# Placing a pair's late tiles over the last tile's y, leaving one attention slot empty, and re-pacing background steps in a fused attention, MoE and MoE kernel

## The chip, the core and the metric

One core of a Trainium2 chip runs the whole program. The metric is the device time of one execution in microseconds (us), median of several executions.

## The reference

Attention over short windows, then two feed-forward blocks in a row, all in float32:

```python
# attention: 4 x 8 heads, 768 positions, 64 wide; chunks of 32 see 16 left, 8 right, 8 memory keys
scores = scale * q_c @ k_full.T; a = exp(scores - max); out = (a / sum) @ v_full
x = out as [3072 tokens, 512]
# first MoE block (512 -> 1536 -> 512)
xn = x / rms(x) * rms_g
x = (silu(xn @ w_gate) * (xn @ w_val)) @ w_out
# second MoE block (512 -> 2048 -> 512)
h = x @ w_in;  g = h if h >= 1, 0 if h <= -1, else (h + 1)**2 / 4
return g @ w_out
```

## The kernel before

The 3072 tokens are six tiles of 512. A float32 product is made of three matmuls on operands split into a high and a low part, so nearly all of TensorE's work comes in threes.

Part one: a hand-written order of attention for the first tile. Part two: the first MoE block for tiles 0 to 3, one at a time (the loop over t, lines 793 to 822). For each of 12 blocks f of the hidden width it runs 12 matmuls for the gate (into ps_g[0], then Silu on ScalarE), 12 for the value (into ps_g[1], then VectorE multiplies and splits the product into hh and hl), and 12 for the output of the block before (out1, into ps_y). Each block has three slots, one behind each of these steps: s = 3f, 3f+1 and 3f+2. In a slot the kernel issues, in this order, a step of attention for later tiles (att_slot), a step that makes operands for the pair that follows (xq, from x_steps) and some background steps (conv_step), which split the second block's weights. At f = 11 it splits the next tile's x behind the value matmuls (split_x, four copies on ScalarE and four subtractions on VectorE), ahead of slot 34. After the last block evacuate copies ps_y to the tile ys and a DMA writes it to y_d.

Attention works on pairs of units. A pair has nine steps at fixed distances (plan2): s (scores), a (transpose of the exponentials), v (values), each twice, r (norm), x (transpose), twice; pairs follow each other at 11 slots. All steps use one PSUM tile, ps_a, so each has to wait until VectorE or ScalarE has read what the step before left there.

Part three: tiles 4 and 5 go through the first MoE block together (proj1 and out1p, lines 997 to 1008). A block f takes seven products of six matmuls each in place of eight (product, lines 829 to 840), and then 12 matmuls of out1p. Part four is the second MoE block for three such pairs (proj2, out2), from about 718 us to the end.

Background steps are a list of 328 entries. For each of 32 weight units the list has c (ScalarE), join two entries later (three VectorE instructions, lines 132 to 140), hi (ScalarE) one later, lo (VectorE and a DMA of POOL's queue) two later, and the load of the unit three ahead (POOL's queue) five later; every fourth unit adds sums over two entries, and hi and lo parts of these sums. Units start seven entries apart. conv_step(n) takes n entries on average; slot takes 2, 7/3 or 3 and product takes 1.

From t = 1 on every engine's order is the order written here: ScalarE, VectorE, POOL and SP each work off one list, and an instruction that waits holds all behind it. Tiles of a pool that is opened where another was closed wait for the last use of what lay in their place. The pool p1 of part three lies where the pools of part two lay: first xs with the tile "xn" (8 KB of each partition; its last user is ys), then x high and low parts, hh, hl and s. p1 hands out places in the order of the calls: p0 to p6 (2 KB each), e1 (4 KB), four wo (4 KB each), s12 and s34.

Of the kernel before, what the change touches and what calls it, by code (L numbers as in the profile page):

```python
# [8 lines left out]
F32 = mybir.dt.float32  # L9
# [7 lines left out]
P = 128  # L17
# [14 lines left out]
TT = 512  # L32
# [6 lines left out]
def tile_stream_attention_moe_moe2(  # L39
# [14 lines left out]
    KK = DM // P  # L54
    NTT = NT // TT
# [3 lines left out]
    pool = lambda name, bufs, **kw: ctx.enter_context(tc.tile_pool(name=name, bufs=bufs, **kw))  # L59
    const = pool("const", 1)  # L60
    wpool = pool("wpool", 1)
    att_only = ctx.enter_context(ExitStack())
# [13 lines left out]
    xs = poolS("xs", 1)  # L76
# [21 lines left out]
    x_d = {t: dram.tile([P, KK, TT], F32, name=f"x_d{t}") for t in range(2, NTT)}  # L98
    NS = NTT - 2
# [152 lines left out]
    def w2_steps(g):  # L252

        dp, do = w2p_d[g], w2o_d[g]
        f32_, S = {}, []

        part = lambda j, n: w2raw[j][:, 512 * n:512 * n + 512]

        def c(j):
            f32_[j] = tmp.tile([P, 512], U32, tag="tu", name="tu")  # L260
            nc.scalar.activation(f32_[j].bitcast(F32), words(w2raw[j])[1].bitcast(F32), AF.Copy, scale=2.0 ** -112)

        def hi(j, n):
            nc.scalar.activation(part(j, 0)[:, n:].bitcast(F32R), f32_[j].bitcast(F32)[:, n:], AF.Copy)

        def lo(j, n, dst):
            tt_(
                out=part(j, 1)[:, n:].bitcast(F32),
                in0=f32_[j].bitcast(F32)[:, n:],
                in1=part(j, 0)[:, n:].bitcast(F32),  # L270
                op=ALU.subtract,
            )
            src = w2raw[j].bitcast(F32).rearrange("p (h c) -> p h c", h=2)
            nc.gpsimd.dma_start(dst, src[:, :, n:])

        dsts = [dp[:, :, 0:2].rearrange("p h k c -> p h (k c)"), dp[:, :, 2], do[:, :, 0], do[:, :, 1]]
        for k in range(4):
            j, n = 4 * g + k, W2 + 28 * g + 7 * k
            n0 = 256 if k == 1 else 0
            at(n, lambda j=j: c(j))  # L280
            at(n + 2, lambda j=j: join(f32_[j], w2raw[j]))
            at(n + 3, lambda j=j, n0=n0: hi(j, n0))
            at(n + 5, lambda j=j, n0=n0, k=k: lo(j, n0, dsts[k]))
            at(n + 10, lambda j=j: load_w2(j + 3))
        a, b, n = 4 * g, 4 * g + 1, W2 + 28 * g

        def first():
            if m2["single"]:
                S.extend([sp.tile([P, TT], F32, tag="s", name="s12"), sums_.tile([P, TT], F32, tag="s34", name="s34")])
            else:  # L290
                S.extend(m2["pool"].tile([P, TT], F32, tag=x, name=x) for x in ("s12", "s34"))
            S[:] = [x.rearrange("p (k c) -> p k c", k=2) for x in S]
            live.append(g)
            sums(S, two(f32_[a]), two(f32_[b]), True)

        at(n + 10, first)
        at(n + 11, lambda: sums(S, two(f32_[a]), two(f32_[b]), False))
        at(n + 12, lambda: hi_s(S, 0, f32_[a]))
        at(n + 13, lambda: hi_s(S, 1, f32_[b]))
        at(n + 14, lambda: lo_s(S, 0, f32_[a], dp))  # L300
        at(n + 15, lambda: (lo_s(S, 1, f32_[b], dp), live.remove(g)))

    m2 = {"single": True, "pace": 0.0}
# [234 lines left out]
    def proj_in(ps, unit):  # L538
        wh, wl = unit
        for kk in range(KK):  # L540
            sl = slice(kk * P, (kk + 1) * P)
            mm3(ps, (wh[:, sl], wl[:, sl]), xhl[kk], kk == 0, kk == KK - 1)
# [52 lines left out]
    for st in ORDER.split():  # L595
# [4 lines left out]
        n = int(n)  # L600
# [62 lines left out]


    plan2 = {0: "s0", 2: "a0", 3: "s1", 4: "v0", 5: "a1", 7: "v1", 9: "r0", 10: "x0", 12: "x1"}

    def att_slot(t, s):
        if t == 0:
            o, r = divmod(s, 18)
            if r in plan:  # L670
                att_step(2 + o, plan[r])
            return
        s += 36 * (t - 1)
        for pr in range(4, 2 * NTT):
            st = plan2.get(s - 11 * (pr - 4))
            if st is not None:
                att_step(pr, st)

# [24 lines left out]
    def conv_step(n):  # L703
        m2["pace"] += n
        while m2["pace"] >= 1:
            m2["pace"] -= 1
            for fn in bg.pop() if bg else ():
                fn()

    def slot(t, s):  # L710
        att_slot(t, s)
        if t == 0:
            conv_w()
            load_w(units1, 1)
        else:
            if xq:
                xq.pop(0)()

            n = 36 * t - 36 + s
            conv_step(2 if n < 48 else 7 / 3 if n < 88 else 3)  # L720

    xn_t.pop(0)
    pend = None
# [13 lines left out]
    def load_y(*src):  # L737
        for o in range(2):
            nc.sync.dma_start(m2["y"][:, o], src[o])
# [23 lines left out]
    def x_steps(e):  # L763
        y = m2["y"]
        B11, B21, B12, B22 = y[:, 0, 0:2], y[:, 0, 2:4], y[:, 1, 0:2], y[:, 1, 2:4]
        tt = nc.vector.tensor_tensor

        def hi(c, x):
            nc.scalar.activation(xb[:, 2 * c:2 * c + 2, 0], x, AF.Copy)

        def lo(c, x):
            tt(
                out=xb[:, 2 * c:2 * c + 2, 1],
                in0=x,
                in1=xb[:, 2 * c:2 * c + 2, 0].bitcast(F32),
                op=ALU.subtract,
            )


        yield lambda: tt(out=e, in0=B12, in1=B11, op=ALU.subtract)  # L780
        yield lambda: tt(out=B12, in0=B22, in1=B12, op=ALU.subtract)
        yield lambda: (hi(0, B11), hi(2, e))
        yield lambda: (lo(0, B11), hi(3, B12))
        yield lambda: (tt(out=B11, in0=B12, in1=B11, op=ALU.add), hi(1, B11))
        yield lambda: (lo(1, B11), hi(4, B21))
        yield lambda: (lo(2, e), hi(5, B22))
        yield lambda: lo(3, B12)
        yield lambda: lo(4, B21)
        yield lambda: (tt(out=B21, in0=B21, in1=B11, op=ALU.subtract), hi(6, B21))
        yield lambda: lo(5, B22)  # L790
        yield lambda: lo(6, B21)

    for t in range(NS):
        if t == 1:
            region.close()
            region.enter_context(tc.manual_schedule())
        for f in range(F1):
            if t == NS - 1 and f == 6:
                att_only.close()
                right = ctx.enter_context(tc.tile_pool(name="right", bufs=1, side="right", reuse_waits="tile"))  # L800
                m2["y"] = right.tile([P, 2, KK, TT], F32, name="y")
                load_y(x_d[NS], x_d[NS + 1])
            if t == NS - 1 and f == 7:
                xq.extend(x_steps(xs.tile([P, 2, TT], F32, tag="xn", name="e")))
            if 0 < t < NS - 1 and f == 9:
                load_x(t + 1)
            if t == NS - 1 and f == F1 - 1:
                load_wp(0)
            proj_in(ps_g[0], w1[("g", f)])
            s = sp.tile([P, TT], F32, tag="s", name="s")  # L810
            nc.scalar.activation(s, ps_g[0], AF.Silu)  # L811
            slot(t, 3 * f)
            proj_in(ps_g[1], w1[("v", f)])
            if f == F1 - 1 and t + 1 < NS:
                split_x(xn_t.pop(t + 1))
            nc.vector.tensor_tensor(out=s, in0=s, in1=ps_g[1], op=ALU.mult)
            split_h(f, s, nc.gpsimd if t == 0 else nc.vector)
            slot(t, 3 * f + 1)
            if pend is not None:
                out1(*pend)  # L820
            pend = (t, f)
            slot(t, 3 * f + 2)
# [6 lines left out]
    def product(n, bank, a, x, start):  # L829

        for kk in range(2):
            sl = slice(kk * P, kk * P + P)
            wh, wl = (wp[:, n % 2, i, a, sl] for i in range(2))
            xh, xl = (xb[:, 2 * x + kk, i] for i in range(2))
            st = start and kk == 0
            nc.tensor.matmul(bank, wh, xh, start=st, stop=False, skip_group_check=True)  # L836
            nc.tensor.matmul(bank, wh, xl, start=False, stop=False, skip_group_check=True)  # L837
            nc.tensor.matmul(bank, wl, xh, start=False, stop=kk == 1, skip_group_check=True)  # L838
        if x:
            conv_step(1)  # L840

    def tmp2(name):
        m2["n"] += 1
# [141 lines left out]
    single_only.close()  # L985
    pair1 = moe1_only.enter_context(ExitStack())
    m2["pool"] = pair1.enter_context(tc.tile_pool(name="p1", bufs=1, reuse_waits="tile"))
    m2["t"], m2["n"] = [m2["pool"].tile([P, TT], F32, name=f"p{i}") for i in range(7)], 0
    m2["e"] = m2["pool"].tile([P, 2, TT], F32, name="e1")
    pair_bank.close()  # L990
    bpool = ctx.enter_context(
        tc.tile_pool(name="bpool", bufs=1, space=bass.MemoryType.PSUM, side="right", reuse_waits="tile")
# [128 lines left out]
```

## Time and profile before

| | us |
|---|---|
| median of 3 runs | 1215.93 (1214.59 to 1216.49) |
| the profiled execution's own time | 1213.37 |
| its span | 1211.6 |
| TensorE busy in it | 1169.8 |
| VectorE busy | 761.2 |
| ScalarE busy | 496.8 |

The span runs from the first to the last instruction. A matmul's end is modelled and overlaps the next one, so a hole in TensorE's work is best read from the starts of two neighbours.

### The profile page before, as it was taken

What the parts mean: (1) busy time and instruction counts of PE and PEld (TensorE: products, weight loads), DVE (VectorE), ACT (ScalarE), POOL (GpSimd) and SP (SyncE); (2) the same over time, 40 slices, a digit from 0 to 9 for tenths busy, and PEclk for the clock granted to TensorE, in tenths of its full rate; (3) what the DMA queues carried; (4) which work ended last, traced back from release to release, by engine and by line L of the source; (5) the groups of instructions that cost most, each with busy time, mean ns of one, the idle gap of its engine ahead of it and who ended that gap; (6) DMA issues with size and microseconds to landing.
All of it is one profiled execution on the core that took longest, in us unless ns stands there. A gap on an engine that the chain in (4) does not pass through costs nothing.

```text
span 1211.6 us, 19907 instructions
## 1 busy us (share of the span) xinstructions
PE 1169.8 (97%) x7993; PEld 940.8 (78%) x7993; DVE 761.2 (63%) x1256; ACT 496.8 (41%) x830; POOL 171.2 (14%) x219
## 2 busy tenths in 40 slices
PE   7888899999999999889999999999999999999998
PEld 4666677777777778668888788888888888888887
DVE  5898856656656665866767728666176664466620
ACT  4665655455544653433333414334043332233310
POOL 2655421121221212212101000000000000000000
PEclk8898999999999999989999999999999999999999
DMA  8555538887957666489787766756565656555354
GB/s 300 181 187 179 185 113 276 289 287 252 327 178 232 208 230 219 177 319 322 284 355 267 291 226 237 266 195 243 198 223 197 260 199 219 198 209 191 131 191 156
DMA packets 98061, 278.60 MB, mean 230 GB/s; under 512 B 10032, under 2 KB 22320, under 8 KB 91568
## 3 DMA queue, kind: packets, MB, share of 16 engines
q1 hardware_dynamic: 79408, 218.59, 51.5%
q0 software_dynamic: 15104, 52.44, 12.1%
q10 hardware_dynamic: 3456, 6.29, 1.4%
q8 instruction: 63, 1.03, 0.3%
q14 instruction: 30, 0.25, 0.1%
HBM read 209.13 MB, written 68.16 MB: 229 GB/s over the span
## 4 chain that ended last, share of the span: by engine, by line
PE 54%; DMA 2%; DVE 2%; ACT 0%; issue 0%; POOL 0%; SPq 0%; DVEq 0%; ACTq 0%
PE ps_y L975 7%; PE ps_y L974 7%; PE ps_y L973 7%; PE ps_b L836 5%; PE ps_b L837 5%; PE ps_b L838 5%; PE ps_g L836 4%; PE ps_g L838 4%; PE ps_g L837 4%; PE ps_y L535 2%; PE ps_y L536 2%; PE ps_y L534 2%; DMA w<-in_w_dram 1%; DMA wo<-w1o_d 1%; DMA y_d<-ys 1%
## 5 line engine op out<-in xcount | busy, mean ns | idle before, releaser
L534 PE MATMUL ps_g<-xh,wall 128*128 128x512 f32 x384 | 159.3, 415 | 3.3 <-ACT s L811 2.2
L536 PE MATMUL ps_g<-xh,wall 128*128 128x512 f32 x384 | 153.6, 400 | 0.0
L535 PE MATMUL ps_g<-xl,wall 128*128 128x512 f32 x384 | 153.4, 400 | 0.0
L973 PE MATMUL ps_y<-wo,wall 128*128 128x512 f32 x324 | 126.0, 389 | 0.0
L974 PE MATMUL ps_y<-wo,wall 128*128 128x512 f32 x324 | 126.0, 389 | 0.0
L975 PE MATMUL ps_y<-wo,wall 128*128 128x512 f32 x324 | 126.0, 389 | 0.0
L897 ACT ACTIVATE t<-t,half 128x512 f32<-128x512 f32 x96 | 69.0, 720 | 132.0 <-DVE t L896 132.0
L836 PE MATMUL ps_b<-wall 128*128 128x512 f32 x288 | 112.8, 392 | 0.2 <-DVE p L869 0.2
L837 PE MATMUL ps_b<-wall 128*128 128x512 f32 x288 | 112.5, 391 | 0.0
L838 PE MATMUL ps_b<-wall 128*128 128x512 f32 x288 | 112.4, 390 | 0.0
L534 PEld LDWEIGHTS ps_g<-xh,wall 128*128 128x128 f32 x384 | 73.6, 192 | 21.9 <-ACT s L811 3.1
L836 PE MATMUL ps_g<-wall 128*128 128x512 f32 x216 | 84.5, 391 | 3.5 <-ACT p L863 3.5
L911 DVE TENSOR_TENSOR t<-t,ps_g 128x512 f32<-128x512 f32 x24 | 16.5, 688 | 112.6 <-PE ps_g L838 107.7
L536 PEld LDWEIGHTS ps_g<-xh,wall 128*128 128x128 f32 x384 | 73.2, 191 | 17.8
L535 PEld LDWEIGHTS ps_g<-xl,wall 128*128 128x128 f32 x384 | 73.7, 192 | 15.4
L838 PE MATMUL ps_g<-wall 128*128 128x512 f32 x216 | 84.3, 390 | 0.0
L837 PE MATMUL ps_g<-wall 128*128 128x512 f32 x216 | 84.3, 390 | 0.0
L534 PE MATMUL ps_y<-hh,wall 128*128 128x512 f32 x192 | 78.7, 410 | 1.0 <-ACT hh L106 1.0
L535 PE MATMUL ps_y<-hl,wall 128*128 128x512 f32 x192 | 75.9, 396 | 0.2 <-DVE hl L107 0.2
L536 PE MATMUL ps_y<-hh,wall 128*128 128x512 f32 x192 | 76.0, 396 | 0.0
L974 PEld LDWEIGHTS ps_y<-wo,wall 128*128 128x128 f32 x324 | 60.8, 188 | 12.7
L973 PEld LDWEIGHTS ps_y<-wo,wall 128*128 128x128 f32 x324 | 60.8, 188 | 12.6
(155 smaller groups left out, 2304.5 us busy)
## 6 DMA issues: line engine op xcount, KB each, us to landing
wo<-w2o_d SPq DMA_DIRECT2D x100, 512.0 KB, 4.7
wall<-w2p_d SPq DMA_DIRECT2D x24, 1792.0 KB, 7.4
wall<-w1p_d SPq DMA_DIRECT2D x12, 1792.0 KB, 8.8
w<-in_w_dram SPq DMA_DIRECT2D x36, 512.0 KB, 4.1
w<-in_w_dram POOLq DMA_DIRECT2D x32, 512.0 KB, 5.6
k_in<-in_k_dram SPq DMA_DIRECT2D x48, 256.0 KB, 4.4
wo<-w1o_d SPq DMA_DIRECT2D x24, 512.0 KB, 7.4
v_in<-in_v_dram SPq DMA_DIRECT2D x40, 260.0 KB, 4.1
```

Of the source, the lines that this page charges most:

```text
L534: nc.tensor.matmul(ps, wh, xh, start=start, stop=False)
L535: nc.tensor.matmul(ps, wh, xl, start=False, stop=False)
L536: nc.tensor.matmul(ps, wl, xh, start=False, stop=stop)
L836: nc.tensor.matmul(bank, wh, xh, start=st, stop=False, skip_group_check=True)
L837: nc.tensor.matmul(bank, wh, xl, start=False, stop=False, skip_group_check=True)
L838: nc.tensor.matmul(bank, wl, xh, start=False, stop=kk == 1, skip_group_check=True)
L897: nc.scalar.activation(s, s, AF.Square, scale=0.5, bias=half)
L911: tt(out=u2, in0=a, in1=b2, op=ALU.add)
L973: nc.tensor.matmul(ps_y[m], hi[:, sl], wh, start=b == 0, stop=False)
L974: nc.tensor.matmul(ps_y[m], hi[:, sl], wl, start=False, stop=False)
L975: nc.tensor.matmul(ps_y[m], lo[:, sl], wh, start=False, stop=b == F2 - 1)
```

## The change

- The slot behind split_x (s = 34 of tiles 1 and 2, and of tile 3) gets no attention step. All later steps move back by one slot, those behind the second such place by two. The last pair's last step comes one slot earlier relative to its pair (11 in place of 12). 
- Background entries: 2 in a slot up to slot 47, 7/3 from 48 to 89, then 2; before it was 7/3 from 48 to 87, then 3. product takes one entry for each of its seven calls, before for six.
- The load of the pair's x (load_y) stands behind slot 18 of tile 3 and not ahead of block 6; x_steps are queued behind slot 21 and not ahead of block 7.
- In p1, e1 and a new tile s1234 (4 KB, in place of s12 and s34) are allocated first, p0 to p6 behind them.

```diff
@@ w2_steps, first
-                S.extend(m2["pool"].tile([P, TT], F32, tag=x, name=x) for x in ("s12", "s34"))
+                S.extend(m2["late"][:, i] for i in range(2))
@@ att_slot
+    plan3 = {11 if r == 12 else r: st for r, st in plan2.items()}
+        if s == 34:
+            return
         s += 36 * (t - 1)
+        s -= (s > 34) + (s > 70)
         for pr in range(4, 2 * NTT):
-            st = plan2.get(s - 11 * (pr - 4))
+            st = (plan3 if pr == 2 * NTT - 1 else plan2).get(s - 11 * (pr - 4))
@@ slot
-            conv_step(2 if n < 48 else 7 / 3 if n < 88 else 3)
+            conv_step(7 / 3 if 48 <= n < 90 else 2)
@@ loop over f: moved from ahead of proj_in(ps_g[0], ...) to behind slot(t, 3 * f)
+            if t == NS - 1 and f == 6:
+                att_only.close()
+                right = ctx.enter_context(tc.tile_pool(name="right", bufs=1, side="right", reuse_waits="tile"))
+                m2["y"] = right.tile([P, 2, KK, TT], F32, name="y")
+                load_y(x_d[NS], x_d[NS + 1])
+            if t == NS - 1 and f == 7:
+                xq.extend(x_steps(xs.tile([P, 2, TT], F32, tag="xn", name="e")))
@@ product
-        if x:
-            conv_step(1)
+        conv_step(1)
@@ p1
+    m2["e"] = m2["pool"].tile([P, 2, TT], F32, name="e1")
+    m2["late"] = m2["pool"].tile([P, 2, TT], F32, name="s1234")
     m2["t"], m2["n"] = [m2["pool"].tile([P, TT], F32, name=f"p{i}") for i in range(7)], 0
-    m2["e"] = m2["pool"].tile([P, 2, TT], F32, name="e1")
```

## Rows read from the trace of the kernel before

**Rows 1.** The page's part 1: busy time, share of the span, instructions.

```profile
PE 1169.8 (97%) x7993; PEld 940.8 (78%) x7993; DVE 761.2 (63%) x1256; ACT 496.8 (41%) x830; POOL 171.2 (14%) x219
```

**Rows 2.** Waits of PE, whole span: us in total, times, longest.

```profile
PE ps_g L534 <- ACT s L811: 2.2, 2, 2.0
```

**Rows 3.** Timeline of PE, the pair's start: start, us, line, names [idle before].

```profile
533.96 0.39 PE L837 MATMUL ps_b<-wall 128*128 128x512 f32 x1
534.19 0.39 PE L838 MATMUL ps_b<-wall 128*128 128x512 f32 x1
538.04 0.50 PE L836 MATMUL ps_g<-wall 128*128 128x512 f32 x1 [3.46 <-ACT p L863]
...
542.30 0.39 PE L838 MATMUL ps_b<-wall 128*128 128x512 f32 x1
```

**Rows 4.** Windows: length, busy PE, PEld, DVE, ACT, POOL, then clock, DMA, GB/s.

```profile
540.40:542.40 2.00, 2.00 (x6) 1.54 (x6) 1.30 (x3) 1.60 (x3) 0.00 (x0) 0.53 1.02 410
```

**Rows 5.** Timelines of SP and of ACT at the pair's start.

```profile
529.94 0.32 SPq L568 DMA_DIRECT2D y_d<-ys  x1
...
537.39 0.60 ACT L863 ACTIVATE p<-ps_g 128x512 f32<-128x512 f32 x1 [7.97 <-DMA y_d<-ys]
```

**Rows 6.** Timeline of PE, blocks 10 and 11 of tile 3.

```profile
506.55 0.49 PE L534 MATMUL ps_g<-xh,wall 128*128 128x512 f32 x1 [1.13 <-DVE s L816]
...
514.40 0.50 PE L534 MATMUL ps_g<-xh,wall 128*128 128x512 f32 x1 [1.99 <-ACT s L811]
...
518.38 0.40 PE L535 MATMUL ps_g<-xl,wall 128*128 128x512 f32 x1
...
525.57 0.50 PE L534 MATMUL ps_y<-hh,wall 128*128 128x512 f32 x1 [0.96 <-ACT hh L106]
526.30 0.50 PE L535 MATMUL ps_y<-hl,wall 128*128 128x512 f32 x1 [0.23 <-DVE hl L107]
```

**Rows 7.** Windows, columns as in rows 4: late tile 3; the pair.

```profile
498.00:515.50 17.50, 14.38 (x60) 10.97 (x59) 15.82 (x24) 9.02 (x14) 5.00 (x9) 0.98 0.53 180
...
542.00:680.00 138.00, 137.83 (x604) 112.81 (x602) 96.53 (x158) 48.86 (x83) 18.57 (x31) 1.00 0.81 297
```

**Rows 8.** Instructions of DVE by line, 484 to 530 us: busy us, mean ns, idle before.

```profile
L772 DVE TENSOR_TENSOR wall<-y,wall 128x1024 fp32r<-128x1024 f32 x6 | 7.3, 1221 | 0.8 <-ACT wall L769 0.8
L135 DVE SCALAR_TENSOR_TENSOR tu<-w,tu 128x512 uint32<-128x512 uint32 x6 | 4.2, 693 | 0.2
...
L132 DVE TENSOR_SCALAR tu<-tu 128x512 uint32<-128x512 uint32 x7 | 3.0, 423 | 1.1 <-ACT tu L261 1.1
```

**Rows 9.** Timeline of ACT, the hi step ahead of block 10's Silu.

```profile
513.24 0.63 ACT L264 ACTIVATE w<-tu 128x512 fp32r<-128x512 f32 x1 [4.99 <-issue]
```

**Rows 10.** Timeline of PE, between tiles 1 and 2.

```profile
287.06 0.65 PE L421 MATMUL ps_a<-ident,e 128*128 128x128 f32 x4 [1.61 <-ACT x_nat L523]
```

**Rows 11.** Timelines of PE and of DVE, between tiles 2 and 3.

```profile
410.06 0.63 PE L421 MATMUL ps_a<-ident,e 128*128 128x128 f32 x4 [2.15 <-DVE x_nat L464]
...
408.12 0.69 DVE L107 TENSOR_TENSOR hl<-s,hh 128x512 fp32r<-128x512 f32 x1 [0.70 <-ACT hh L106]
```

**Rows 12.** Timelines of PE, DVE, ACT: pair 11's second s to second a.

```profile
439.06 0.86 PE L391 MATMUL ps_a<-k_in,q_in 64*32 64x64 f32 x64
...
446.54 0.60 PE L421 MATMUL ps_a<-ident,e 128*128 128x128 f32 x4
...
440.03 0.69 DVE L404 TENSOR_REDUCE m<-ps_a 128x8 f32<-128x512 f32 x1 [1.60 <-PE ps_a L391]
...
445.03 0.76 DVE L464 TENSOR_TENSOR x_nat<-ps_a,rd 128x256 f32<-128x256 f32 x2
...
442.69 1.28 ACT L811 ACT_TABLE_LOAD   x1
443.99 0.60 ACT L811 ACTIVATE s<-ps_g 128x512 f32<-128x512 f32 x1
```

**Rows 13.** Line 745 (load_wp), its issues: landing times.

```profile
DMA to landing us min/median/max: 6.9/7.5/9.9
```

More of the change, by code (lines that the diff above doesn't have):

```diff
@@ L797, in tile_stream_attention_moe_moe2 @@
         for f in range(F1):
[L798 to L804, printed above, removed]
             if 0 < t < NS - 1 and f == 9:
```

## The prediction

> **What bounds the kernel now.** I read the busy times first. TensorE is busy for 97% of the span [rows 1], so the most that an edit which adds and removes no matmul can give is what TensorE idles, and what it runs at the lower clock. Next I read its waits and its timeline, and looked for neighbours whose starts lie further apart than 0.23 us, the spacing of two matmuls in a full run [rows 3]. From 718 us to the end there is no such place worth naming, and the first 140 us are not touched. What is left is four places: two at tile boundaries, one in the last third of tile 3, one at the start of the pair. A hole costs the idle time shown in the row plus 0.16, since a matmul is drawn 0.39 to 0.40 long and the next could start 0.23 behind it.
>
> **A. The start of the pair.** TensorE stands for 3.46 us behind ScalarE's first copy of proj1, line 863 [rows 3], and that copy waited 7.97 us for the DMA y_d<-ys [rows 5]. The DMA was issued at 529.94 and the copy ran at 537.39. The reader is to see that the copy doesn't read ys: it writes p1, which lies where ys lay. By the order of places the first 8 KB are p0 to p3, and all four are among the first that proj1 writes. The hole costs 3.46 + 0.16 = 3.6 us. Behind it the granted clock is 0.53 [rows 4], the lower level (1.2 GHz). From 538.04 to 542.30 TensorE starts 11 matmuls in 4.26 us where 11 x 0.233 = 2.56 would do [rows 3], so 1.7 more. A is 5.3 us. With the change e1 and s1234 fill these 8 KB. s1234 is first written by the sums of unit group 5, and e1 at the pair's end. The p tiles now lie over x parts whose last reader is tile 3's last value matmul, 5.6 us (24 x 0.233) ahead of the pair, and ScalarE's copy has only its own queue ahead of it: the last hi and two copies of evacuate. By my count of VectorE's and ScalarE's lists the copy then runs about 2.7 us into the pair, and its PSUM bank is wanted again after four products, 24 x 0.233 = 5.6 us. What is next late is one of two SP matters. The four wo now lie over hh, hl and s; s12 of group 4 sits in one of the s, and its store is now among the last of tile 3. But the first wo is wanted only after two blocks of products, 84 x 0.233 = 19.6 us. And the first weights of the pair (load_wp(0)) leave when block 9's output is done; up to the pair that is one block and one out1, 48 x 0.233 = 11.2 us, against landings of 6.9 to 9.9 [rows 13]. Cover of 1.3 us at the worst row. I take all of A, 5.3; the ends are 0 (another wait of the same length) and 5.3.
>
> **B. The last third of tile 3.** VectorE is busy for 15.82 of 17.5 us there [rows 7], and three engines wait on it in turn: hi waits 4.99 us behind join [rows 9], block 10's Silu stands behind hi in ScalarE's list, and TensorE waits for that Silu [rows 6]. Holes: 1.13, 1.99 and 0.96, each plus 0.16 [rows 6], make 4.6; the Silu wait is counted twice with 2.2 in all [rows 2], so a second hole of 0.2 + 0.16 = 0.4; 525.57 to 526.30 is 0.73 for one matmul, 0.5 too much; and from 514.40 to 518.38 ten matmuls took 3.98 in place of 2.33, 1.65 for the lower clock behind the hole. B is 7.1 us.
>
> Why VectorE is late can be counted. An x step is 1.22 (line 772), join is 0.42 + 0.69 + 0.69 = 1.8 (lines 132 and 135, the third like the second), lo and each of the two late sums' parts 0.69, a half-width sum 0.42 [rows 8]; multiply, wait for hh, and hl are 2.1 a block. TensorE needs 36 x 0.233 = 8.4 us a block. Before, with three entries a slot: block 8 has three x steps, two joins and a lo: 10.1; block 9 three x steps, four sums, a half lo, two parts, a join: 11.1; block 10 three x steps, a join, two lo: 9.0. That is 30.2 for 25.2 of TensorE. With two entries a slot and the x steps one slot later: block 7 has two x steps, a join, a lo: 7.0; block 8 the same; block 9 three x steps, a join, a lo: 8.3; block 10 three x steps, a join, four sums: 9.3; block 11 one x step, a half lo, two parts, a join: 6.9. Only block 10 is over, by 0.9, and the blocks before it leave room. Followed through the list, block 11's multiply comes some 0.7 us behind its operands and hl just as out1 wants it; I leave 0.3 of B standing and take 6.8. The ends are 3.4 (VectorE's lateness stays by half) and 7.1. The moved load_y stays where it was on SP, directly behind the store of the last x; load and first x step both move by about a slot, so VectorE's wait for y stays about as it was. It holds the next multiply only if it lasts more than the room of block 7, 8.4 - 7.0 = 1.4 us longer.
>
> **Where the taken entries go.** Tile 1 to 3 now do 230 entries in place of 249; product does 84 in place of 72; 14 are left at the pair's end in place of 7. In the pair VectorE is busy for 96.53 of 138 us [rows 7]; a group of 28 entries is about 12.8 us of it (four joins, lo, the sums), 0.46 an entry, so 12 more are 5.5 us, 74% in place of 70%. No price on TensorE. The seven left at the end add a join and a lo, 2.5 us, ahead of the x steps of the second block; 144 matmuls of out1p, 33.6 us, hide them; without that cover they would cost 2.5.
>
> **C. Between tiles 1 and 2.** The x transpose of slot 34 leaves ps_a to a ScalarE copy (line 523) that stands behind four copies of split_x and hh. TensorE's next attention step waits 1.61 [rows 10]: 1.8 us. Now the transpose is in slot 35, 12 matmuls later, with the next step another 12 later. The copy needs no VectorE work any more. I leave 0.1 and take 1.7; the ends are 0 and 1.8.
>
> **D. Between tiles 2 and 3.** Here slot 34 held a v step whose readers on VectorE stood behind the four subtractions and hl (end at 408.12 + 0.69 = 408.8, [rows 11]). TensorE waited 2.15 [rows 11]: 2.3 us. This one moves in part only. Slots 35, 36, 37 now hold s, v, a, in neighbouring slots, and the slot of s also has c and join, which VectorE does ahead of v's readers. Pair 11 had this very sequence before: from the start of s, VectorE took it up after 0.97, v's readers ended after 6.73 (445.03 + 0.76), and a started after 7.48 with no wait [rows 12], so 0.75 of room. Now s starts at 410.06 - 2.31 - 0.8 = 406.95 on the old clock (the hole and v's place gone), and VectorE, which has hl and a lo ahead, takes it up at 409.4, 2.45 after in place of 0.97. 1.5 later with 0.75 of room, and 0.1 on v: 0.9 us of hole stay, and I take 1.4. The ends are -0.5 and 2.3.
>
> Pair 11's s to a also shows a table load: 442.69, 1.28 long, its activation at 443.99, 0.02 behind its end [rows 12]. The Trainium skill (ScalarE: Activation LUTs, section What ACT_TABLE_LOAD costs) puts a drain of 1.38 behind every load of 1.28, 2.66 together; the row shows none. With it D would give nothing and the time would be 1202.1; without, it is the sum below.
>
> **The other attention steps** shift by one or two slots against the blocks. I price that at nought, with -0.5 and +0.5 as ends: half the room of pair 11 and more than any of their waits.
>
> **Sum.** 5.3 + 6.8 + 1.7 + 1.4 = 15.2 us. The profiled execution took 1213.37 around its span of 1211.6, so it would take 1198.2 with a span of 1196.4. The median of the runs is 2.56 above the profiled one: 1215.93 - 15.2 = **1200.7**.
>
> **The rivals.**
> - Tile 3 stays late by half (chance 0.13). VectorE's list is a queue, and block 10 is over its time by count; a late load of a weight unit or of y would hold all of it. For it speaks that y's wait moves with it; against it the sums. 1200.7 + 3.4 = 1204.1.
> - The attention holes only move (0.08): C and D give nothing, 1200.7 + 3.1 = 1203.8. For it speaks that D already shows a hole in the new place.
> - Only D's exponential is late (0.05): its table load starts once VectorE is done and not ahead of it, 1.28 later, and D gives 0.1. 1202.0. By the page's drain it would be the same place and about the same price.
> - The pair's start gets another wait in place of the old (0.07): load_wp(0) with 1.3 of cover, now leaving beside POOL's stores, or the late tiles don't cover ys as stated. 1200.7 + 5.3 = 1206.0.
> - Slower than before (0.03): in the pair an entry for each of seven products, with units seven entries apart, puts join into the same place of every block, behind the sixth product, ahead of gate1's sum and what frees the third bank. If each of 12 joins held TensorE for its 1.8 us, that is 21.7: 1222.4. It decides from 15.2 / 12 = 1.27 us a block. Against it: bank three is wanted again only after two products and an out1p, 18 matmuls and more.
>
> **How the numbers follow.** The forecast has 0.64, 1200.7. The range reaches down to all holes gone (1.3 less) and the spread of the runs, 1198.0, and up past the dearest of the rivals that are still faster, 1207.0. A measurement of this kernel tells about 0.2% (2.4 us) from no change. All cases but the slower one are faster by over 0.2%: faster 0.95, same 0.02, slower 0.03.
>
> **What would show it.** Right: the first copy of proj1 waits for its product and not for a DMA, and no matmul of 0.63 follows (A); no wait of TensorE for Silu or the multiply in blocks 9 to 11, and VectorE with gaps between 498 and 515 (B); no wait between tiles 1 and 2 (C); one of about 1 us between tiles 2 and 3 (D). Wrong: a DMA among TensorE's or ScalarE's releasers at the pair's start; a weight unit's load that c waits for; TensorE waiting in the pair for VectorE in every block.

## The result, and the profile after

The changed kernel takes 1204.9 us (median of 4 runs, 1204.48 to 1208.11) against 1215.83 (median of 4) before: a ratio of 0.991, 95% interval 0.9886 to 0.9934. That is 10.9 us where 15.2 were forecast. 1204.9 lies inside the range, 4.2 above the forecast. The profiled execution has a span of 1202.4 in place of 1211.6.

The waits of TensorE over the span (us in total, times, longest) no longer have the rows of [rows 2], nor those behind [rows 3, 6, 10, 11]. Two others are new; in the first, 2.0 of the 5.8 belong to the start of the kernel, where a wait of 1.9 stood before.

```profile
PE ps_a L391 <- DMA q_in<-in_q_dram: 5.8, 2, 3.8
...
PE ps_g L841 <- DMA wall<-w1p_d: 0.8, 1, 0.8
```

The timeline of TensorE in tile 2 shows the larger one. Line 391 is a scores step: pair 8's second s, in slot 48.

```profile
328.93 0.40 PE L536 MATMUL ps_g<-xh,wall 128*128 128x512 f32 x1
333.15 1.17 PE L391 MATMUL ps_a<-k_in,q_in 64*32 64x64 f32 x64 [3.82 <-DMA q_in<-in_q_dram]
334.25 0.79 PE L534 MATMUL ps_g<-xh,wall 128*128 128x512 f32 x1
...
338.25 0.40 PE L534 MATMUL ps_g<-xh,wall 128*128 128x512 f32 x1
```

The hole costs 3.82 + 0.16 = 4.0. Behind it the s step took 1.10 to the next matmul in place of 0.79 (the v step from 339.05 to 339.84), and nine matmuls took 4.00 where 9 x 0.233 = 2.10 would do; the windows (columns as in rows 4) give the clock.

```profile
332.00:336.00 4.00, 2.85 (x68) 2.42 (x69) 1.38 (x2) 0.07 (x1) 0.54 (x1) 0.50 0.39 134
...
505.50:523.00 17.50, 17.50 (x76) 13.99 (x75) 15.39 (x24) 6.82 (x11) 2.48 (x4) 1.00 0.53 207
```

0.50 is the lower level. In all 4.0 + 0.3 + 1.9 = 6.2 us are lost there. The second row answers to [rows 7]: in the last third of tile 3 VectorE is still busy for 15.39 of 17.5 us, but TensorE for all of it, at full clock.

At the pair's start ScalarE's first copy runs 1.85 us after the pair's first matmul (524.88) and names no DMA; compare [rows 5]. The weights that block 2 waits for are those of load_wp(2).

```profile
526.73 0.60 ACT L867 ACTIVATE p<-ps_g 128x512 f32<-128x512 f32 x1
...
547.68 0.47 PE L841 MATMUL ps_g<-wall 128*128 128x512 f32 x1 [0.77 <-DMA wall<-w1p_d]
```

| Place | forecast gain | in the trace |
|---|---|---|
| A, the pair's start | 5.3 | 5.3, then 0.9 lost at block 2 |
| B, tile 3 | 6.8 | 7.1 |
| C, between tiles 1 and 2 | 1.7 | 1.8 |
| D, between tiles 2 and 3 | 1.4 | 2.3 |
| other attention steps | 0 | -6.2 |

16.5 - 0.9 - 6.2 = 9.4, against 9.2 in the spans.

### The profile page after: what moved, and what is told of

It is laid out like the page before. It is cut to its first block, busy times and chain, and to the rows that moved or that the text cites. A ratio compares the mean times of both kernels' runs of the same rounds, so it can differ in the third digit from the quotient of the medians.

```text
span 1202.4 us, 19908 instructions
## 1 busy us (share of the span) xinstructions
PE 1166.8 (97%) x7993; PEld 941.1 (78%) x7993; DVE 761.5 (63%) x1256; ACT 496.2 (41%) x830; POOL 170.1 (14%) x219
## 4 chain that ended last, share of the span: by engine, by line
PE 87%; DVE 6%; DMA 3%; issue 2%; ACT 2%; SPq 0%; POOL 0%; DVEq 0%; ACTq 0%; POOLq 0%
PE ps_y L979 7%; PE ps_y L978 7%; PE ps_y L977 7%; PE ps_g L534 7%; PE ps_g L536 6%; PE ps_g L535 6%; PE ps_b L843 5%; PE ps_b L841 5%; PE ps_b L842 5%; PE ps_y L534 5%; PE ps_y L535 5%; PE ps_y L536 5%; PE ps_g L841 4%; PE ps_g L843 4%; PE ps_g L842 4%
## 5 line engine op out<-in xcount | busy, mean ns | idle before, releaser
L534 PEld LDWEIGHTS ps_g<-xh,wall 128*128 128x128 f32 x384 | 73.9, 193 | 17.4 <-issue 0.2
L915 DVE TENSOR_TENSOR t<-t,ps_g 128x512 f32<-128x512 f32 x24 | 16.5, 687 | 111.7 <-PE ps_g L843 106.6
```

What stands on the lines that cost most here:

```text
L534: nc.tensor.matmul(ps, wh, xh, start=start, stop=False)
L915: tt(out=u2, in0=a, in1=b2, op=ALU.add)
```

## Where the new hole comes from

Keys and queries of a unit go into single buffers, so their load is issued in the slot of the s step before. SP's queue around pair 8's first s, changed kernel; lines 218 to 220 are the three stores of the last unit of the first block's weights (512, 256 and 512 KB):

```profile
317.49 0.63 SPq L218 DMA_DIRECT2D w1p_d<-wall  x1
318.17 0.99 SPq L219 DMA_DIRECT2D w1p_d<-wall  x1
319.26 1.28 SPq L220 DMA_DIRECT2D w1o_d<-wall  x1
320.63 2.43 SPq L357 DMA_DIRECT2D k_in<-in_k_dram  x2
323.12 1.52 SPq L358 DMA_DIRECT2D q_in<-in_q_dram  x1
```

The same in the kernel before:

```profile
317.40 0.83 SPq L357 DMA_DIRECT2D k_in<-in_k_dram  x2
318.28 0.45 SPq L358 DMA_DIRECT2D q_in<-in_q_dram  x1
318.82 0.53 SPq L218 DMA_DIRECT2D w1p_d<-wall  x1
```

Before, the first s and the stores were both in slot 44, and a slot issues attention first. The change moves s to slot 45; the stores, an entry of the background list, stay in slot 44. The query load lands 9.9 us after its issue at 323.12, that is at 333.0, and s starts at 333.15. In the trace of before the same load landed 6.6 after its issue, at 324.9, and s started at 327.06 without a wait. At the same time POOL loads 1 MB of the second block's weights (line 248); these are its issues, first in the changed kernel, then in the kernel before:

```profile
318.26 0.55 POOL L248 DMA_DIRECT2D w<-in_w_dram  x1 [0.50 <-issue]
321.12 0.53 POOL L248 DMA_DIRECT2D w<-in_w_dram  x1 [2.32 <-DMA w1p_d<-s]
...
317.89 0.55 POOL L248 DMA_DIRECT2D w<-in_w_dram  x1 [0.50 <-issue]
320.00 0.55 POOL L248 DMA_DIRECT2D w<-in_w_dram  x1 [1.55 <-DMA w1p_d<-s]
```

So there were two theories: the order on SP (S), or full DMA engines whatever the order (W).

Each of the experiments was timed beside the kernel before, whose median there was 1215.64 us for e1 to e4 and 1217.76 for e5 to e8; gains are therefore taken from the ratios, each with its 95% interval.

**e1_align.** The changed kernel; the background list is held back by a slot too, and caught up:

```diff
-            conv_step(7 / 3 if 48 <= n < 90 else 2)
+            conv_step(7 / 3 if 48 <= n < 90 else 0 if n == 34 else 4 if n == 47 else 2)
```

> The changed kernel, but slot 34 takes no background entries either and slot 47 takes four, so each attention step from slot 35 to 46 meets the entries that it met before. Theory S (the load of keys and queries for pair 8's second s stands on SP behind the three stores, 1.28 MB, of the last w1 unit, and so lands late): in slot 45 the load is issued ahead of the stores again; the hole of 3.8 us at that s and the slow matmuls behind it (5.9 us in all) are gone, 1199 us, 0.995 of the changed kernel. Rival W (the DMA engines are full there whatever the order, with POOL's two weight loads of 512 KB beside): the bytes and their slots are the same, so the hole stays, 1205 us.

Measured 1199.36 us, 0.9857 of the kernel before (0.9837 to 0.9878), apart from the changed kernel's interval. That is 17.4 us. SP's queue, POOL's loads and the s step (no wait):

```profile
320.62 1.14 SPq L357 DMA_DIRECT2D k_in<-in_k_dram  x2
321.80 0.47 SPq L358 DMA_DIRECT2D q_in<-in_q_dram  x1
322.38 0.53 SPq L218 DMA_DIRECT2D w1p_d<-wall  x1
...
322.86 0.55 POOL L248 DMA_DIRECT2D w<-in_w_dram  x1 [2.85 <-DMA w1p_d<-wgv]
324.16 0.54 POOL L248 DMA_DIRECT2D w<-in_w_dram  x1 [0.76 <-DMA w1p_d<-s]
...
330.28 0.86 PE L391 MATMUL ps_a<-k_in,q_in 64*32 64x64 f32 x64
```

The query load lands 5.7 us after its issue, and the hole is gone, as S had it. But this run doesn't part S from W: holding the list back moved POOL's two loads too. In the changed kernel both are issued ahead of the query load, here both behind it. Only e2 and e3 part the theories. This is also the best kernel of the study, with e8_align_wo.

**e2_w2_later.** The changed kernel; SP's order stays wrong, POOL's loads come later:

```diff
-    at(W2 - 8, lambda: (load_w2(0), load_w2(1)))
+    at(W2 - 4, lambda: (load_w2(0), load_w2(1)))
```

> The changed kernel, but POOL's first two loads of the second block's weights (1 MB) come four entries later, behind the load that pair 8's second s waits for. Rival W: the hole goes or shrinks to under 1 us, about 1200 us. Theory S: the load is still behind 1.28 MB of stores on SP; the hole shrinks at most by the share of the DMA engines that POOL's 1 MB took (1 MB at 400 GB/s is 2.5 us, of which less than half falls before the landing), so 2 to 4 us of the hole stay, 1203 to 1205 us.

Measured 1200.3 us, 0.9873 (0.9847 to 0.9898), and no hole:

```profile
317.06 1.29 SPq L220 DMA_DIRECT2D w1o_d<-wall  x1
318.46 1.99 SPq L357 DMA_DIRECT2D k_in<-in_k_dram  x2
320.50 0.93 SPq L358 DMA_DIRECT2D q_in<-in_q_dram  x1
...
326.06 0.55 POOL L248 DMA_DIRECT2D w<-in_w_dram  x1 [0.48 <-DMA x_d<-x_nat]
326.80 0.54 POOL L248 DMA_DIRECT2D w<-in_w_dram  x1 [0.19 <-DMA x_d<-x_nat]
...
327.07 0.86 PE L391 MATMUL ps_a<-k_in,q_in 64*32 64x64 f32 x64
```

The query load is still behind the stores, but lands after 5.0 us, at 325.5, with 1.6 to spare. S by itself falls: I had expected 2 to 4 us of the hole to stay. The place behind the stores makes no hole while POOL's loads are not beside them.

**e3_swap_before.** The kernel before; in slot 44 alone the background entries are issued ahead of attention:

```diff
     def slot(t, s):
+        n = 36 * t - 36 + s
+        if n == 44:
+            conv_step(2)
         att_slot(t, s)
```

(The later call is left out for n = 44.)

> The kernel before, but in slot 44 alone the background entries are issued ahead of the attention step, so that the same load stands behind the three stores. Same bytes, same slots. Theory S: a hole of about 3 to 5 us appears at pair 8's second s (slot 47), with slow matmuls behind it: 1219 to 1222 us, over 0.3% slower. Rival W: no hole, 1216 us.

Measured 1220.72 us, 1.0038 (1.0025 to 1.0051): 4.6 us slower. The hole is there, with eight slow matmuls behind it:

```profile
323.40 1.65 SPq L358 DMA_DIRECT2D q_in<-in_q_dram  x1
...
320.13 0.55 POOL L248 DMA_DIRECT2D w<-in_w_dram  x1 [0.50 <-issue]
323.78 0.54 POOL L248 DMA_DIRECT2D w<-in_w_dram  x1 [3.10 <-DMA w1p_d<-s]
...
331.95 0.85 PE L391 MATMUL ps_a<-k_in,q_in 64*32 64x64 f32 x64 [2.57 <-DMA q_in<-in_q_dram]
```

No attention step was moved here, and POOL's list is that of before: the edit changes only an order, and with the order of before there is no hole, so W as stated falls. Counted from the store of line 525 ahead of it in the queue (315.63 before, 317.87 here), the query load is issued 2.9 us later, and it lands 8.4 us after its issue in place of 6.6. Of these 4.7 us before had 2.2 to spare; 2.5 are left, the hole.

Together e2 and e3 show that it takes both, the place behind the stores and POOL's loads beside them, and that either one taken away is enough. The Trainium skill (DMA: Bandwidth & Descriptors, section Queues, rings and completion order) says that each DMA engine consumes a ring's descriptors in order and takes turns between the queue rows that have work for it. e3 against before agrees with the first half (8.4 us behind the stores, 6.6 ahead of them), e2 against the changed kernel with the second (5.0 us without POOL's loads beside, 9.9 with them).

## The parts one by one

**e4_no_attention.** The changed kernel without its attention part, load_y and x steps as before:

```diff
-        if s == 34:
-            return
-        s -= (s > 34) + (s > 70)
```

> The changed kernel with attention, load_y and the x steps where they were before: only the place of the late tiles and the pace are changed. If the parts add up: A's 5.3 us and B's 7.1 us are won, the two boundary holes (1.8 and 2.3) stay, and the new hole of 5.9 is not there: 1215.8 - 12.4 = 1203.4 us, a little under the changed kernel. Theory S says that the new hole belongs to the attention part, so it must be absent here; if it belonged to the pace it would be present (1209 us).

Measured 1202.38 us, 0.9887 (0.9864 to 0.991), 1.0 under the sum of the parts. With its attention part the change was not faster (0.991, 0.9886 to 0.9934). The waits at the two boundaries stand as before and the new one is absent:

```profile
PE ps_a L421 <- DVE x_nat L464: 2.2, 1, 2.2
PE ps_a L421 <- ACT x_nat L523: 1.6, 1, 1.6
PE ps_g L836 <- DMA wall<-w1p_d: 1.2, 1, 1.2
```

**e5_layout.** The kernel before, with e1 and s1234 allocated first in p1 and nothing else:

```diff
+    m2["e"] = m2["pool"].tile([P, 2, TT], F32, name="e1")
+    m2["late"] = m2["pool"].tile([P, 2, TT], F32, name="s1234")
     m2["t"], m2["n"] = [m2["pool"].tile([P, TT], F32, name=f"p{i}") for i in range(7)], 0
```

> The kernel before with the place of the late tiles changed and nothing else. Theory (term A): the hole of 3.5 us at the pair's start and the slow matmuls behind it go, all else stays: 1215.6 - 5.3 = 1210.3 us. Rival: ScalarE's queue or the first weights of the pair hold the same place, the hole stays in part: 1213 to 1215 us.

Measured 1214.45 us, 0.9974 (0.9959 to 0.9989): 3.2 us (1.3 to 5.0) of the 5.3. The theory's 5.3 lies just outside, and the rival's 0.6 to 2.6 are in part inside. In the trace it is VectorE that waits for ys, though ScalarE's queue, which the rival named, has a part in it. Timelines of VectorE, TensorE and ScalarE:

```profile
542.38 0.43 DVE L187 TENSOR_TENSOR s<-tu 128x256 f32<-128x256 f32 x1 [3.76 <-DMA y_d<-ys]
...
543.79 0.80 PE L836 MATMUL ps_b<-wall 128*128 128x512 f32 x1 [4.52 <-DVE p L869]
...
535.44 0.66 ACT L261 ACTIVATE tu<-w 128x512 f32<-128x512 f32 x1 [7.00 <-DMA w<-in_w_dram]
```

The wait for ys has moved to the late tile. With the old pace the sums of unit group 5 are entry 250, taken in block 0 of the pair. They write s1234, which now lies over ys, and hold VectorE's list. With the new pace entry 250 comes in block 2. In the same trace c waits 7.0 us for a weight unit at the pair's start and holds ys's own copies behind it. That is not the layout's doing: the same wait is 7.3 us in e3 and 8.9 in e7, which have the old layout and the old pace, and 1.7 in the trace of before; in no trace with the new pace is it over 0.7. So with the new pace a second wait at this place is gone, of which the trace of before shows little.

This profiled execution took 1219.19 us, 4.7 above the median of its ten. Its pair's start loses 0.63 and 4.52 us, no less than in before, so it shows how the wait can move and not where the 3.2 us come from. That A gives its whole 5.3 is shown only together with the new pace (the changed kernel and e4).

**e6_pace.** The kernel before, with the new counts in slot and product and nothing else:

```diff
-            conv_step(2 if n < 48 else 7 / 3 if n < 88 else 3)
+            conv_step(7 / 3 if 48 <= n < 90 else 2)
-        if x:
-            conv_step(1)
+        conv_step(1)
```

> The kernel before with the pace of the background entries changed and nothing else. Theory (term B): the holes in blocks 8 to 11 of tile 3 go and those at the boundaries and at the pair's start stay: 1215.6 - 7.1 = 1208.5 us. Rival: what the last third of tile 3 gives back is waited for at the pair's start, since the store of ys then meets more traffic: the hole there grows by some us and the gain is 3 to 5 us, 1211 to 1213 us.

Measured 1209.06 us, 0.993 (0.9913 to 0.9946), 8.5 us by the ratio (6.6 to 10.6). Tile 3 has no hole left; the one at the pair's start is longer than in [rows 3], 5.0 in place of 3.5:

```profile
PE ps_g L836 <- ACT p L862: 5.0, 1, 5.0
```

So B is right in size, and the rival's 3 to 5 us lie outside. The longer hole doesn't speak for the rival either: with the old pace e3 and e7 show 6.2 us at this place.

```profile
PE ps_g L839 <- ACT p L866: 6.2, 1, 6.2
...
PE ps_g L840 <- ACT p L867: 6.2, 1, 6.2
```

Its length varies from trace to trace, from 3.5 to 6.2.

**e7_attention.** The kernel before, with plan3, the empty slot, load_y and x steps moved:

```diff
+        if s == 34:
+            return
         s += 36 * (t - 1)
+        s -= (s > 34) + (s > 70)
```

> The kernel before with the attention steps, load_y and the x steps moved and nothing else. Theory (order of the stores and POOL's loads together): the two boundary holes (1.8 and 2.3) go, the hole at pair 8's second s comes (4 to 6 us): 1215.6 - 4.1 + 4 to 6 = 1215.5 to 1217.5 us, so this part is worth nothing by itself, or costs. By the prediction (C and D as priced, the rest of the shift at nought) it would be 1212.5 us.

Measured 1217.73 us, 0.9996 (0.9978 to 1.0013): nothing (from 1.6 slower to 2.7 faster), as the theory had it, and not the 3.1 us of C and D. The waits of TensorE from 150 to 740 us have lost both boundary rows and got

```profile
PE ps_a L391 <- DMA q_in<-in_q_dram: 2.5, 1, 2.5
```

**e8_align_wo.** As e1_align, and half of the pair's first output weights later:

```diff
-    for i in range(4):
-        load_wo(i)
+    for i in range(2):
+        load_wo(i)
     for f in range(F1):
         proj1(f)
+        if f == 0:
+            for i in range(2, 4):
+                load_wo(i)
```

> As e1_align, and the third and fourth load of the pair's output weights (1 MB) are issued behind block 0's products and not ahead of them. Theory: the last hole of the pair's start (about 1 us at block 2, TensorE waiting for the weights that SP loads behind these) is made by 2 MB of output weights queued ahead of them; with 1 MB less ahead it goes: 1 us under e1_align, 1198.3 us. Rival: the DMA engines are full there whatever the order; the hole stays, 1199.4 us.

Measured 1199.15 us, 0.9839 (0.982 to 0.9858). The wait at block 2 is gone: from 500 to 560 us TensorE waits for nothing, and the slowest landing of the pair's weights is 10.4 us in place of 13.1 in e1_align. In time it can't be told from e1_align.

```profile
DMA to landing us min/median/max: 6.8/7.5/10.4
```

## Why the prediction was right, and what it missed

- **A** holds in the changed kernel: the hole and the slow matmuls behind it are gone, and ScalarE's copy came 1.85 us into the pair where I had 2.7. What I took for safe, "s1234 is first written by the sums of unit group 5", was true only because the pace moves them; e5 shows the same layout without that. I had doubted load_wp(0), with 1.3 us of cover. It was in time; load_wp(2), which I had not looked at, was 0.8 late behind two megabytes of output weights (e8).
- **B** held by its count. VectorE is as busy as before in the last third, yet one block at most is over its 8.4 us, and the 0.3 that I left standing isn't there.
- **C** held: 1.8, with no wait left there.
- **D** gave 2.3 where I left a hole of 0.9. The step that failed is the start of VectorE's work: I kept the old time of split_x. Before, its copies stood on ScalarE behind an exponential and a hi and began 0.4 us (403.67) ahead of the step behind the value matmuls (404.06). Now the slot ahead of it holds an a step, whose copy is short, and they begin 1.0 ahead (407.06 and 408.09). So s was taken up 412.73 - 410.98 = 1.75 after its start and not 2.45, v's readers ended at 417.65 + 0.76 = 418.41, and a started at 418.55:

```profile
412.73 0.68 DVE L404 TENSOR_REDUCE m<-ps_a 128x8 f32<-128x512 f32 x1
417.65 0.76 DVE L464 TENSOR_TENSOR x_nat<-ps_a,rd 128x256 f32<-128x256 f32 x2
...
418.55 0.63 PE L421 MATMUL ps_a<-ident,e 128*128 128x128 f32 x4
```

- **The other attention steps** are the term that was wrong: priced at nought with 0.5 either way, they cost 6.2. I had followed these steps on TensorE, VectorE and ScalarE and against ps_a only. An s step also issues a load of 768 KB on SP, and the shift moved it past 1.28 MB of stores while POOL was loading 1 MB. Neither the sum nor a rival had that queue, though the stores and the load stand in the code within one slot of each other.
- The forecast's other errors (D 0.9, B 0.3, C 0.1 too low, block 2's wait of 0.9 not seen) nearly cancel.
- Part of the nearness is luck. The time lies inside the range because its upper end was set by rivals that did not happen. And the sum carried over 2.56 us between the profiled execution and the median as if the change left them alone; in the changed kernel they are 0.4 (1204.48 and 1204.9). Between the profiled executions the change gave 8.9 us and not 15.2, between the medians 10.9. A likely reason, not shown with one trace a kernel, is that the trace of before, from which A and B were read, was a light one: e3 and e7 with the same layout and pace show 6.2 in place of 3.5 at the pair's start, and 2.2 and 2.7 in place of 0.96 ahead of tile 3's last out1.

Left open: what sets the length of the hole at the pair's start in the old layout. In e6 the copy waits for y_d<-ys as before; that this store meets more traffic was only argued, and e3 and e7 have a longer hole without e6's pace.

## What to carry to other kernels

When a step is moved by one place, list what it issues on every queue, and check each DMA against the transfers that it now stands behind; here a load that had 2.2 us to spare came too late behind 1.28 MB of stores, with 1 MB of another queue beside them. Where a list of background work and a list of foreground steps share a queue, shift both or neither. A tile that is laid over a late store must be late itself under the schedule that it is used with, not under the one that it was drawn for.

## What the runs showed of the hardware

Loads behind stores on SP also took longer to issue: two key loads 0.83 us ahead of the stores (before) and 2.43 behind them (the changed kernel), and the query load 0.45 and 1.52, before any landing time. Why is not shown. In the trace of before a single hole of 2.15 us [rows 11] was followed by matmuls at full spacing (granted clock 1.00 from 410 to 414 us), and one of 1.99 us that began 5.9 us behind the end of another of 1.13 [rows 6] by ten matmuls with 1.65 us lost (0.57 from 514.4 to 518.4). So of these two the longer hole was not the one that cost clock.
